# V products of two tiles in one run of TensorE, in a fused attention and MLP kernel on one Trainium2 core

## The chip, the core and the metric

The kernel runs on one core of one Trainium2 chip. The metric is the device time of one execution in microseconds (us); lower is better. The core has TensorE (PE in the profile, with its weight loads as PEld), VectorE (DVE), ScalarE (ACT), GpSimd (POOL) and SyncE (SP), which issues most DMAs. Each engine works through its own list of instructions in order, and they wait for one another by semaphores. Matrix products land in PSUM, which GpSimd does not read here; everything else lies in SBUF.

## The reference, cut to what matters

```python
q_assign = np.argmax(np.einsum('bhsd,hcd->bhsc', q_n, c_n), axis=-1)   # 16 clusters per head
k_assign = np.argmax(np.einsum('bhsd,hcd->bhsc', k_n, c_n), axis=-1)
mask = q_assign[:, :, :, None] == k_assign[:, :, None, :]
scores = np.where(mask, scale * np.matmul(q, k.transpose(0, 1, 3, 2)), -1e9)
attn = np.exp(scores - np.max(scores, axis=-1, keepdims=True))
x = np.matmul(attn / (np.sum(attn, axis=-1, keepdims=True) + 1e-09), v)
...
u = x + np.real(np.fft.fft(np.fft.fft(x, axis=1), axis=2))
un = (u - mean) / np.sqrt(var + 1e-6)
x = u + np.maximum(un @ w_ch1, 0.0) @ w_ch2                             # 512 -> 2048 -> 512
...
h = np.maximum(x @ w_in, 0.0)                                           # 512 -> 1024
out = (h * sigmoid(conv3(h))) @ w_out                                   # 3 taps along the sequence
```

There are 2 batches, 8 heads, 768 tokens and 64 columns per head. A head is masked attention over 768 keys; the batch's heads together are the 512 columns of the MLP stages.

## The kernel before

**Tiles and steps.** The 16 heads (2 batches of 8) are cut into 6 tiles of 128 rows each, 96 tiles in all. One loop of steps `n` works on all of them, skewed: step n makes the scores of tile n+8 with queries as rows (`score_max`, tiles named `s`; VectorE takes the row maxima `m6`), the transposed scores of tile n (`score_exp`, tiles named `t`; ScalarE takes the exponential `p`), splits the exponential of tile n-1 into a high f16 part (`prob_hi`, ScalarE) and a low one (`prob_lo`, GpSimd, or VectorE for the tiles in the set `LO_ON_DVE`), and multiplies tile n-3 with V (`attn_v`, 18 matmuls of 65 columns). Scores are two passes over f32 stacks `X` and `Y`, which hold a head's high and low parts, the mask rows and the maxima.

**The queue of PSUM slots.** `s` and `t` share three PSUM slots in turn, so each `s` or `t` waits until the tile three places earlier has been read: an `s` by VectorE's maximum, a `t` by ScalarE's exponential.

**What is hung into the steps.** All other work of the stage has a place in a step by a table: `at(where, step, ...)` gives the usual one and `MOVED` overrides it. The places within a step are, in this order: `pre`, `mid` (between the `s` matmuls and the maximum), `mid2` (after the `t` matmuls), `late` (before `prob_lo`), then V products, then `aft`, `post` and `fill`. For every pair of heads m (12 steps) this is: `prep_sims`, `sims_turn`, `equal_turn` and `equal_sole` make the cluster mask (matmuls, a ScalarE copy `eT`, VectorE maxima and comparisons); `prep_hi` and `prep_lo` split q and k into the tile `G`; `v_max`, `v_turn` and `v_step` scale and split V; `max_turn` (step 6h-2) transposes the maxima of head h and sends them by DMA into `Y`; `attn_out` divides by the row sums; `prep_stack` (step 6h-12) moves a head's parts from `G` into its stacks by five DMAs on SP, needed by the `s` of step 6h-8; `ahead_start`, `ahead` and `ahead_store` fetch and convert the first MLP weights. From step 52 on, the DFT of the first batch (`mixing`) and its normalisation (`norm`) are hung in too.

**The end of the stage.** After step 88 the last exponentials are split, and the first MLP weights are split into parts by `first_split(0)` to `first_split(3)` on VectorE: parts 0 and 1 (`firstEH`, `firstEL`) feed the up product `first_up`, parts 2 and 3 (`firstYsH`, `firstYsL`) the down product, which comes after both up products. The exponentials of tiles 89, 93 and 95 stay in their PSUM slot until their low part is taken (`IN_PLACE`). After this the MLP stages run, with their own order, which the change leaves alone.

Of the kernel before, what the change touches and what calls it, by code (L numbers as in the profile page):

```python
# [21 lines left out]
B, H, S, D = 2, 8, 768, 64  # L22

DFT_LOADS = (9, 20, 21, 32, 33, 44)
LO_ON_DVE = {4, 5, 6, 7, 8, 14, 16, 19, 20, 28, 31, 32, 40, 43, 44, 52, 55, 57, 59, 61, 67, 68, 72, 77, 80,
             82, 85, 88, 90, 92}
# [6 lines left out]
MOVED = {  # L33
    ("prep_sims", 2): ("post", 5),
    ("equal_turn", 2): ("mid", 7),
    ("equal_sole", 2, 0): ("mid", 8),
    ("prep_hi20", 2): ("late", 8),
    ("equal_sole", 2, 1): ("mid", 9),
    ("prep_hi21", 2): ("fill", 9),
    ("prep_lo", 2, 0): ("pre", 9),  # L40
    ("attn_out", 0, 0): ("fill", 10),
    ("attn_out", 0, 1): ("fill", 10),
    ("attn_out", 0, 2): ("fill", 11),
    ("prep_lo", 2, 1): ("late", 11),
    ("v_max", 2): ("aft", 11),
    ("v_step", 1, 0): ("late", 11),
    ("v_step", 1, 1): ("aft", 11),
    ("v_turn", 1): ("mid", 11),
    ("v_step", 1, 2): ("pre", 12),
    ("v_step", 1, 3): ("late", 12),  # L50
    ("v_step", 1, 4): ("late", 13),
    ("v_step", 1, 5): ("aft", 14),
    ("ahead_start", 0): ("fill", 15),
    ("attn_out", 1, 0): ("fill", 15),
    ("v_step", 2, 0): ("late", 15),
    ("v_turn", 2): ("mid", 15),
    ("v_step", 2, 1): ("late", 16),
    ("v_step", 2, 2): ("aft", 16),
    ("v_step", 2, 3): ("fill", 16),
    ("ahead0_1",): ("fill", 17),  # L60
    ("attn_out", 1, 2): ("pre", 17),
    ("prep_sims", 3): ("post", 17),
    ("v_step", 2, 4): ("fill", 17),
    ("prep_hi30", 3): ("late", 20),
    ("prep_hi31", 3): ("late", 20),
    ("v_step", 2, 5): ("fill", 20),
    ("prep_lo", 3, 0): ("late", 21),
    ("attn_out", 2, 1): ("late", 22),
    ("prep_lo", 3, 1): ("pre", 22),
    ("attn_out", 2, 2): ("fill", 23),  # L70
    ("ahead0_3",): ("fill", 24),
    ("v_max", 3): ("late", 25),
    ("attn_out", 3, 0): ("aft", 26),
    ("ahead_start", 1): ("aft", 27),
    ("ahead_store", 0): ("pre", 27),
    ("v_step", 3, 0): ("late", 27),
    ("v_turn", 3): ("mid", 27),
    ("attn_out", 3, 1): ("late", 28),
    ("v_step", 3, 1): ("late", 28),
    ("v_step", 3, 2): ("aft", 28),  # L80
    ("v_step", 3, 3): ("fill", 28),
    ("ahead1_1",): ("fill", 29),
    ("prep_sims", 4): ("post", 29),
    ("v_step", 3, 4): ("fill", 29),
    ("prep_hi41", 4): ("fill", 32),
    ("v_step", 3, 5): ("fill", 32),
    ("prep_lo", 4, 0): ("late", 33),
    ("attn_out", 4, 1): ("late", 34),
# [40 lines left out]
    ("row",): ("fill", 58),
    ("attn_out", 8, 2): ("fill", 59),  # L130
    ("rowL",): ("fill", 59),
    ("ahead_start", 3): ("late", 60),
# [62 lines left out]
def tile_net(ctx, tc, qk, v, cen, w12, w34, conv, dft, odd, out):  # L195
# [304 lines left out]
    with ExitStack() as actx:  # L500
# [464 lines left out]
        for i, t in enumerate((0, 3, 1, 4, 2, 5)):  # L965
            n = 73 + 3 * i
# [465 lines left out]
```

## Time and profile before

| | us |
|---|---|
| median of 3 runs (671.08 to 673.03) | 672.08 |
| time of the profiled execution | 670.07 |
| its span, first to last instruction | 668.2 |
| PE busy in the span | 655.2 (98%) |
| DVE busy | 525.4 (79%) |
| ACT busy | 424.0 (63%) |
| POOL busy | 179.7 (27%) |
| mean granted TensorE clock, share of full | 0.999 |

The profiled execution spends 1.87 us outside its span and lies 2.0 us under the median of the runs. Matmuls are pipelined in the records: one lasts about 0.34 us but the next starts 0.18 us later, so the distance between starts tells more than the busy time.

### The profile page before, as it was taken

Reading aid. Unit: us, or ns where it says so; the run is one execution under the profiler, and the core shown is the slowest. Engines: PE = TensorE matmul, PEld = TensorE weight load, DVE = VectorE, ACT = ScalarE, POOL = GpSimd, SP = SyncE. Lnnn points to the kernel's source line nnn. Section 1 sums busy time; section 2 is a strip of 40 time slices with the busy share of each in tenths; the row PEclk is TensorE's granted clock in tenths of the full one; section 3 lists DMA queues with packets and bytes.
Section 4 is the critical chain, followed back from the end, with each engine's and each line's share of the span. In section 5 each row is a group of like instructions: output and inputs, shape, how many; then the busy total and the mean of one; then the engine's idle time right before and its main releaser. Section 6 shows DMA issues by size and latency. Waiting matters only on the chain.

```text
span 668.2 us, 12652 instructions
## 1 busy us (share of the span) xinstructions
PE 655.2 (98%) x5041; PEld 486.9 (73%) x5041; DVE 525.4 (79%) x889; ACT 424.0 (63%) x686; POOL 179.7 (27%) x138
## 2 busy tenths in 40 slices
PE   8999999999999999999999999999999999999997
PEld 4888888888898888999989995555555455555553
DVE  6897888788788999996699829998533569987653
ACT  6788888978687894475256734775533466655442
POOL 8445858687569640000011000000000000000000
PEclk9999999999999999999999999999999999999999
DMA  8668887774623810334023330333000000002002
GB/s 222 164 164 207 196 222 210 189 186 100 170 76 74 225 45 2 127 136 179 1 66 124 127 127 0 127 128 126 1 1 1 0 1 1 0 1 95 1 0 95
DMA packets 21543, 65.42 MB, mean 98 GB/s; under 512 B 4438, under 2 KB 7306, under 8 KB 18668
## 3 DMA queue, kind: packets, MB, share of 16 engines
q1 hardware_dynamic: 20476, 60.86, 31.8%
q0 software_dynamic: 1008, 3.75, 2.0%
q8 instruction: 40, 0.66, 0.4%
q14 instruction: 19, 0.16, 0.1%
HBM read 40.84 MB, written 5.58 MB: 69 GB/s over the span
## 4 chain that ended last, share of the span: by engine, by line
PE 72%; DVE 15%; ACT 5%; DMA 3%; issue 2%; SPq 1%; POOL 0%; DVEq 0%; ACTq 0%; POOLq 0%
PE acc L232 8%; PE acc L231 8%; PE acc L230 8%; PE av L870 6%; PE up L230 5%; PE up L231 5%; PE up L232 5%; PE s L790 5%; PE t L830 4%; PE s L792 4%; PE t L832 4%; PE u L230 2%; PE u L232 2%; PE u L231 2%; DVE wa L1138 1%
## 5 line engine op out<-in xcount | busy, mean ns | idle before, releaser
L858 POOL TENSOR_TENSOR p<-p,p 128x768 f16<-128x768 f32 x63 | 107.6, 1718 | 57.8 <-ACT p L850 32.6
L795 DVE TENSOR_REDUCE m<-s 128x1 f32<-128x768 f32 x96 | 90.5, 947 | 17.9 <-PE s L792 7.8
L838 ACT ACTIVATE p<-t,cbias 128x768 f32<-128x768 f32 x93 | 83.6, 900 | 16.2 <-PE t L832 14.8
L850 ACT CAST p<-p 128x768 f16<-128x768 f32 x90 | 74.7, 830 | 1.1
L870 PE MATMUL av<-V,p 128*128 128x65 f16 x1728 | 70.0, 194 | 0.0
L870 PEld LDWEIGHTS <-p 128*128 128x128 f16 x1728 | 58.6, 98 | 15.1 <-issue 15.0
L790 PE MATMUL s<-X 128*128 128x384 f32 x192 | 56.2, 373 | 1.1 <-ACT X L699 0.2
L830 PE MATMUL t<-X 128*128 128x384 f32 x192 | 54.4, 364 | 0.8 <-DVE d L880 0.4
L792 PE MATMUL s<-Y 96*128 96x384 f32 x192 | 49.6, 339 | 0.0
L832 PE MATMUL t<-Y 98*128 98x384 f32 x192 | 49.5, 339 | 0.0
L230 PE MATMUL up<-un,wa 128*128 128x384 f16 x128 | 41.8, 326 | 0.5 <-ACT wa L1137 0.3
L230 PE MATMUL u<-x,wb 128*128 128x384 f16 x128 | 41.7, 326 | 0.1
L231 PE MATMUL up<-un,wa 128*128 128x384 f16 x128 | 41.7, 326 | 0.0
L232 PE MATMUL u<-x,wb 128*128 128x384 f16 x128 | 41.7, 326 | 0.0
L231 PE MATMUL u<-x,wb 128*128 128x384 f16 x128 | 41.7, 326 | 0.0
L232 PE MATMUL up<-un,wa 128*128 128x384 f16 x128 | 41.6, 326 | 0.0
L230 PE MATMUL up<-un,wha 128*128 128x384 f32 x112 | 38.0, 339 | 0.0
L231 PE MATMUL up<-un,wha 128*128 128x384 f32 x112 | 37.8, 338 | 0.0
L232 PE MATMUL up<-un,wla 128*128 128x384 f32 x112 | 37.6, 337 | 0.0
L230 PE MATMUL acc<-wb,gH 128*128 128x512 f16 x96 | 36.4, 379 | 0.2 <-ACT gH L1198 0.2
L230 PE MATMUL acc<-wa,h 128*128 128x512 f16 x96 | 36.4, 379 | 0.0
L231 PE MATMUL acc<-wa,h 128*128 128x512 f16 x96 | 36.4, 379 | 0.0
(404 smaller groups left out, 1653.0 us busy)
## 6 DMA issues: line engine op xcount, KB each, us to landing
rawa<-w SPq DMA_DIRECT2D x14, 1024.0 KB
rawb<-w SPq DMA_DIRECT2D x8, 1024.0 KB
raw<-qk SPq DMA_DIRECT2D x7, 768.0 KB
X<-G SPq DMA_DIRECT2D x13, 384.0 KB
Y<-G SPq DMA_DIRECT2D x13, 384.0 KB
vraw<-v SPq DMA_DIRECT2D x8, 384.0 KB
out<-y SPq DMA_DIRECT2D x12, 256.0 KB
X<-G SPq DMA_DIRECT2D x14, 192.0 KB
```

The lines of the kernel that those rows point to most:

```text
L230: T.matmul(o, sH, mH, start=start, stop=False)
L231: T.matmul(o, sH, mL, start=False, stop=False)
L232: T.matmul(o, sL, mH, start=False, stop=stop)
L790: T.matmul(t[:, c, 0:384], X[:, 0, sl], X[:, 1, 384 * c:384 * c + 384], start=True, stop=False)
L792: T.matmul(t[:, c, 0:384], Y[0:96, 0, sl], Y[0:96, 1, 384 * c:384 * c + 384], start=False, stop=True)
L795: V.tensor_reduce(m6s[h][:, i:i + 1], t[:, :, 0:384], AX.XY, ALU.max, negate=True)
L830: T.matmul(t[:, c, 0:384], X[:, 1, sl], X[:, 0, 384 * c:384 * c + 384], start=True, stop=False)
L832: T.matmul(t[:, c, 0:384], Y[0:98, 1, sl], Y[0:98, 0, 384 * c:384 * c + 384], start=False, stop=True)
L838: A.activation(p, t[:, :, 0:384], AF.Exp, bias=cbias, scale=0.125)
L850: A.copy(p16[:, 0], p32s[n])
L858: eng.tensor_sub(p16[:, 1], p, p16[:, 0])
L870: T.matmul(o, p16[:, k, 128 * j:128 * j + 128], v16[:, i, h % 2, 65 * part:65 * part + 65], start=(i + j + k + part == 0), stop=(i == 5), ...
```

## The change

Up to step 58 (`PAIRED`), V products run only in even steps, and there for two tiles, n-4 and n-3; odd steps have none. After step 58 each step has one tile, as before. The number of matmuls is the same. Besides, `MOVED` gives new places to some 70 small operations, `prob_lo` of tiles 5, 6 and 14 goes from VectorE to GpSimd and that of tile 53 the other way, one `v_max` goes to ScalarE, and `first_split` 1, 2 and 3 go from steps 92, 93 and 95 to 93, 96 and 96.

```diff
-LO_ON_DVE = {4, 5, 6, 7, 8, 14, 16, 19, 20, 28, 31, 32, 40, 43, 44, 52, 55, 57, ...
+LO_ON_DVE = {4, 7, 8, 16, 19, 20, 28, 31, 32, 40, 43, 44, 52, 53, 55, 57, ...
-ABS_ON_ACT = (0, 6)
+ABS_ON_ACT = (0, 1, 6)
 MOVED = {
-    ("prep_sims", 2): ("post", 5),
+    ("prep_sims", 2): ("aft", 5),
+    ("v_max", 1): ("aft", 6),
...
+    ("equal_sole", 3, 0): ("mid2", 20),
...
-    ("v_step", 2, 5): ("fill", 20),
+    ("v_step", 2, 5): ("pre", 19),
...
-    ("ahead_start", 2): ("aft", 37),
+    ("ahead_start", 2): ("aft", 35),
...
-    ("first_split", 2): ("fill", 93),
-    ("first_split", 3): ("fill", 95),
+    ("first_split", 1): ("fill", 93),
+    ("first_split", 2): ("fill", 96),
+    ("first_split", 3): ("fill", 96),
 }
...
-        LEAD, LAG = 8, 3
+        LEAD, LAG, PAIRED = 8, 3, 58
...
-            if 0 <= n - LAG < 88:
-                attn_v(n - LAG)
+            if 0 < n - LAG < 88:
+                for i in (0,) if n > PAIRED else (1, 0) if n % 2 == 0 else ():
+                    attn_v(n - LAG - i)
```

On PE, around steps 25 and 26, the V products (`av` from `p16`, weight load and matmul) stood behind every `t`. Before:

```order
L790 MATMUL s33_1337<-X2_180 128x384 x2
L792 MATMUL s33_1337<-Y2_181 128x384 x2
L830 MATMUL t25_1345<-X1_175 128x384 x2
L832 MATMUL t25_1345<-Y1_176 128x384 x2
L870 LDWEIGHTS p16_22_1266
L870 MATMUL av3_1197<-V16_1_159,p16_22_1266 128x65
L870 LDWEIGHTS p16_22_1266
L870 MATMUL av3_1197<-V16_1_159,p16_22_1266 128x65
```

With the change (its lines lie 17 further down) the same place reads:

```order
L807 MATMUL s33_1337<-X2_180 128x384 x2
L809 MATMUL s33_1337<-Y2_181 128x384 x2
L847 MATMUL t25_1345<-X1_175 128x384 x2
L849 MATMUL t25_1345<-Y1_176 128x384 x2
L807 MATMUL s34_1356<-X2_180 128x384 x2
L809 MATMUL s34_1356<-Y2_181 128x384 x2
L847 MATMUL t26_1364<-X1_175 128x384 x2
L849 MATMUL t26_1364<-Y1_176 128x384 x2
```

The scores of two steps now follow each other, and the V products of tiles 22 and 23 come behind them in one run.

On DVE, at the end of the stage (`first` tiles are the split weights, `p16_93<-t93` is the low part that frees a PSUM slot), the list was:

```order
L1006 TENSOR_TENSOR firstEL_4273<-wa0_4077,firstEH_4195 128x512
L848 CAST p16_92_4275<-p92_4252 128x768
L858 TENSOR_TENSOR p16_92_4275<-p92_4252,p16_92_4275 128x768
L878 TENSOR_SCALAR d14_4302<-av14_4095 128x6
L1008 CAST firstYsH_4304<-wa0_4077 128x512
L856 TENSOR_TENSOR p16_93_4306<-t93_4277,p16_93_4306 128x768
L880 RECIPROCAL d14_4302<-d14_4302 128x6
L848 CAST p16_94_4336<-p94_4313 128x768
L883 SCALAR_TENSOR_TENSOR U_68<-av14_4095,vsc7_3415,d14_4302 128x6x64
L1006 TENSOR_TENSOR firstYsL_4364<-wa0_4077,firstYsH_4304 128x512
```

It is now:

```order
L895 TENSOR_SCALAR d14_4300<-av14_4095 128x6
L1023 TENSOR_TENSOR firstEL_4302<-wa0_4077,firstEH_4195 128x512
L873 TENSOR_TENSOR p16_93_4304<-t93_4275,p16_93_4304 128x768
L897 RECIPROCAL d14_4300<-d14_4300 128x6
L865 CAST p16_94_4334<-p94_4311 128x768
L900 SCALAR_TENSOR_TENSOR U_68<-av14_4095,vsc7_3415,d14_4300 128x6x64
L873 TENSOR_TENSOR p16_95_4362<-t95_4336,p16_95_4362 128x768
L1034 SCALAR_TENSOR_TENSOR firste1_4385<-up0_0_4386,firste0_4384 128x384
L1025 CAST firstYsH_4401<-wa0_4077 128x512
L1023 TENSOR_TENSOR firstYsL_4403<-wa0_4077,firstYsH_4401 128x512
```

The two `firstYs` parts moved behind the low parts of tiles 93 and 95, and `firstEL` behind the cast and the low part of tile 92.

On SP, around step 35 (`mr` sends maxima, the L735 and L728 rows are `prep_stack(8)`), the fetch of MLP weights stood behind the moves:

```order
L805 DMA Y0_139<-mr6_1723 1x6x128 x2
L735 DMA X2_180<-G4_1665 64x1536
L735 DMA X2_180<-G4_1665 32x2x768
L735 DMA Y2_181<-G4_1665 32x2x768
L728 DMA X2_180<-ohd4_1681 16x12x128
L735 DMA Y2_181<-G4_1665 64x2x768
L519 DMA raw5_1798<-qk 128x1536
L981 DMA ahead_950<-w12 128x512
```

It now stands ahead of them:

```order
L822 DMA Y0_139<-mr6_1704 1x6x128 x2
L998 DMA ahead_931<-w12 128x512
L752 DMA X2_180<-G4_1628 64x1536
L752 DMA X2_180<-G4_1628 32x2x768
L752 DMA Y2_181<-G4_1628 32x2x768
L745 DMA X2_180<-ohd4_1680 16x12x128
L752 DMA Y2_181<-G4_1628 64x2x768
L536 DMA raw5_1781<-qk 128x1536
```

The row `ahead<-w12` moved past the five moves of head 8 and past the load of the next q and k.

## Rows read from the trace of the kernel before

**Rows 1.** Page, part 1: busy time, share of span, instructions of each engine.

```profile
PE 655.2 (98%) x5041; PEld 486.9 (73%) x5041; DVE 525.4 (79%) x889; ACT 424.0 (63%) x686; POOL 179.7 (27%) x138
```

**Rows 2.** Windows: stretch, its us, busy PE, PEld, DVE, ACT, POOL, PEclk, DMA, GB/s.

```profile
60.33:156.69 96.36, 94.55 (x1136) 80.99 (x1134) 79.03 (x120) 82.68 (x113) 70.81 (x48) 1.00 0.76 190
239.34:258.83 19.49, 18.19 (x263) 16.22 (x263) 18.16 (x30) 14.68 (x21) 6.42 (x5) 1.00 0.01 3
```

**Rows 3.** Timeline of PE: start, us, what; steps without and with V products.

```profile
24.39 0.52 PE L790 MATMUL s<-X 128*128 128x384 f32 x2
24.75 0.52 PE L792 MATMUL s<-Y 96*128 96x384 f32 x2
...
81.43 0.73 PE L870 MATMUL av<-V,p 128*128 128x65 f16 x18
82.00 0.60 PE L790 MATMUL s<-X 128*128 128x384 f32 x2
82.44 0.51 PE L792 MATMUL s<-Y 96*128 96x384 f32 x2
```

**Rows 4.** Timeline of PE: two tiles' V products in one run, step 95.

```profile
250.62 1.29 PE L870 MATMUL av<-V,p 128*128 128x65 f16 x36
```

**Rows 5.** Timeline, PE and DVE, where PE starts late in steps 18 to 23.

```profile
62.97 0.73 PE L870 MATMUL av<-V,p 128*128 128x65 f16 x18
63.83 0.58 PE L790 MATMUL s<-X 128*128 128x384 f32 x2
...
71.05 0.52 PE L792 MATMUL s<-Y 96*128 96x384 f32 x2
71.74 0.27 PE L800 MATMUL s<-ident,m 128*6 128x128 f32 x1 [0.17 <-DVE m L795]
...
73.40 0.94 DVE L795 TENSOR_REDUCE m<-s 128x1 f32<-128x768 f32 x1
73.55 0.52 PE L792 MATMUL s<-Y 96*128 96x384 f32 x2
74.49 0.59 PE L830 MATMUL t<-X 128*128 128x384 f32 x2 [0.42 <-DVE d L880]
```

**Rows 6.** Timeline, steps 19 to 21: the mask's copy, the maximum, V's low half.

```profile
64.59 0.39 PE L661 MATMUL s<-ident,eq 128*96 128x128 f16 x4
...
65.07 0.58 ACT L664 COPY eT<-s 96x512 f16<-96x512 f16 x1 [0.39 <-PE s L661]
...
65.69 0.96 DVE L795 TENSOR_REDUCE m<-s 128x1 f32<-128x768 f32 x1 [1.14 <-ACT eT L664]
...
69.40 1.01 DVE L772 SCALAR_TENSOR_TENSOR V<-vraw,vsc,V 128x768 f16<-128x768 f32 x1
```

**Rows 7.** Chain that ended last in 60 to 120 us: start, us, what.

```profile
63.07 6.08 DMA Y<-G
```

**Rows 8.** Timeline of PE: last score of step 35, first scores of head 8.

```profile
102.95 0.52 PE L832 MATMUL t<-Y 98*128 98x384 f32 x2
...
112.37 0.60 PE L790 MATMUL s<-X 128*128 128x384 f32 x2
112.98 0.59 PE L792 MATMUL s<-Y 96*128 96x384 f32 x2
```

**Rows 9.** Timeline of DVE, end of the stage.

```profile
247.54 0.68 DVE L432 TENSOR_TENSOR un<-unT,un 128x512 fp32r<-128x512 f32 x1
248.14 1.55 DVE L1006 TENSOR_TENSOR firstEL<-wa,firstEH 128x512 fp32r<-128x512 f32 x1
...
251.15 0.42 DVE L1008 CAST firstYsH<-wa 128x512 fp32r<-128x512 f32 x1
251.48 0.95 DVE L856 TENSOR_TENSOR p<-t,p 128x768 f16<-128x768 f32 x1
```

**Rows 10.** Timeline of POOL and PE in the same stretch.

```profile
247.49 1.65 POOL L858 TENSOR_TENSOR p<-p,p 128x768 f16<-128x768 f32 x1 [4.55 <-ACT p L850]
...
252.58 0.42 PE L230 MATMUL up<-un,firstEH 128*128 128x384 f32 x1 [0.67 <-DVE d L880]
```

More of the change, by code (lines that the diff above doesn't have):

```diff
@@ L24 @@
 DFT_LOADS = (9, 20, 21, 32, 33, 44)
-LO_ON_DVE = {4, 5, 6, 7, 8, 14, 16, 19, 20, 28, 31, 32, 40, 43, 44, 52, 55, 57, 59, 61, 67, 68, 72, 77, 80,
-             82, 85, 88, 90, 92}
+LO_ON_DVE = {4, 7, 8, 16, 19, 20, 28, 31, 32, 40, 43, 44, 52, 53, 55, 57, 59, 61, 67, 68, 72, 77, 80, 82, 85,
+             88, 90, 92}
 AHEAD = 4
@@ L31 @@
 LO_BY_DVE = ()
-ABS_ON_ACT = (0, 6)
+ABS_ON_ACT = (0, 1, 6)
 MOVED = {
-    ("prep_sims", 2): ("post", 5),
+    ("prep_sims", 2): ("aft", 5),
+    ("v_max", 1): ("aft", 6),
     ("equal_turn", 2): ("mid", 7),
-    ("equal_sole", 2, 0): ("mid", 8),
+    ("equal_sole", 2, 0): ("mid2", 8),
     ("prep_hi20", 2): ("late", 8),
+    ("prep_lo", 2, 0): ("fill", 8),
     ("equal_sole", 2, 1): ("mid", 9),
-    ("prep_hi21", 2): ("fill", 9),
-    ("prep_lo", 2, 0): ("pre", 9),
+    ("prep_hi21", 2): ("late", 9),
     ("attn_out", 0, 0): ("fill", 10),
@@ L43 @@
     ("attn_out", 0, 2): ("fill", 11),
-    ("prep_lo", 2, 1): ("late", 11),
+    ("prep_lo", 2, 1): ("pre", 11),
     ("v_max", 2): ("aft", 11),
@@ L49 @@
     ("v_step", 1, 2): ("pre", 12),
-    ("v_step", 1, 3): ("late", 12),
+    ("v_step", 1, 3): ("pre", 12),
     ("v_step", 1, 4): ("late", 13),
@@ L54 @@
     ("attn_out", 1, 0): ("fill", 15),
-    ("v_step", 2, 0): ("late", 15),
+    ("v_step", 2, 0): ("aft", 15),
     ("v_turn", 2): ("mid", 15),
@@ L59 @@
     ("v_step", 2, 3): ("fill", 16),
+    ("ahead0_0",): ("late", 17),
     ("ahead0_1",): ("fill", 17),
-    ("attn_out", 1, 2): ("pre", 17),
-    ("prep_sims", 3): ("post", 17),
+    ("prep_sims", 3): ("aft", 17),
     ("v_step", 2, 4): ("fill", 17),
+    ("ahead0_2",): ("aft", 18),
+    ("attn_out", 1, 2): ("pre", 18),
+    ("v_step", 2, 5): ("pre", 19),
+    ("equal_sole", 3, 0): ("mid2", 20),
     ("prep_hi30", 3): ("late", 20),
     ("prep_hi31", 3): ("late", 20),
-    ("v_step", 2, 5): ("fill", 20),
-    ("prep_lo", 3, 0): ("late", 21),
-    ("attn_out", 2, 1): ("late", 22),
+    ("prep_lo", 3, 0): ("fill", 21),
+    ("attn_out", 2, 1): ("pre", 22),
     ("prep_lo", 3, 1): ("pre", 22),
-    ("attn_out", 2, 2): ("fill", 23),
-    ("ahead0_3",): ("fill", 24),
+    ("ahead0_3",): ("aft", 23),
+    ("attn_out", 2, 2): ("late", 23),
+    ("ahead_start", 1): ("aft", 25),
     ("v_max", 3): ("late", 25),
     ("attn_out", 3, 0): ("aft", 26),
-    ("ahead_start", 1): ("aft", 27),
-    ("ahead_store", 0): ("pre", 27),
-    ("v_step", 3, 0): ("late", 27),
+    ("attn_out", 3, 1): ("late", 27),
+    ("v_step", 3, 0): ("aft", 27),
     ("v_turn", 3): ("mid", 27),
-    ("attn_out", 3, 1): ("late", 28),
     ("v_step", 3, 1): ("late", 28),
@@ L81 @@
     ("v_step", 3, 3): ("fill", 28),
+    ("ahead1_0",): ("late", 29),
     ("ahead1_1",): ("fill", 29),
-    ("prep_sims", 4): ("post", 29),
+    ("prep_sims", 4): ("aft", 29),
     ("v_step", 3, 4): ("fill", 29),
[L85 to L88, printed above, removed]
+    ("ahead1_2",): ("aft", 30),
+    ("ahead_store", 0): ("fill", 30),
+    ("v_step", 3, 5): ("pre", 31),
+    ("equal_sole", 4, 0): ("mid2", 32),
+    ("prep_hi41", 4): ("late", 32),
+    ("prep_hi40", 4): ("aft", 33),
+    ("attn_out", 4, 1): ("pre", 34),
+    ("prep_lo", 4, 0): ("fill", 34),
     ("prep_lo", 4, 1): ("pre", 34),
-    ("attn_out", 4, 2): ("fill", 35),
-    ("ahead1_3",): ("fill", 36),
-    ("ahead_start", 2): ("aft", 37),
-    ("v_max", 4): ("late", 37),
+    ("ahead1_3",): ("aft", 35),
+    ("ahead_start", 2): ("aft", 35),
+    ("attn_out", 4, 2): ("late", 37),
+    ("v_max", 4): ("aft", 37),
     ("attn_out", 5, 0): ("aft", 38),
-    ("v_step", 4, 0): ("late", 39),
+    ("ahead_store", 1): ("fill", 39),
+    ("v_step", 4, 0): ("aft", 39),
     ("v_turn", 4): ("mid", 39),
@@ L100 @@
     ("v_step", 4, 3): ("fill", 40),
+    ("ahead2_0",): ("late", 41),
     ("ahead2_1",): ("fill", 41),
-    ("ahead_store", 1): ("fill", 41),
-    ("prep_sims", 5): ("post", 41),
+    ("prep_sims", 5): ("aft", 41),
     ("v_step", 4, 4): ("fill", 41),
-    ("v_step", 4, 5): ("fill", 44),
+    ("ahead2_2",): ("aft", 42),
+    ("v_step", 4, 5): ("pre", 43),
+    ("equal_sole", 5, 0): ("mid2", 44),
+    ("prep_hi50", 5): ("late", 44),
+    ("attn_out", 6, 1): ("pre", 45),
     ("prep_hi51", 5): ("fill", 45),
-    ("prep_lo", 5, 0): ("late", 45),
-    ("attn_out", 6, 1): ("late", 46),
+    ("prep_lo", 5, 0): ("fill", 45),
     ("prep_lo", 5, 1): ("pre", 46),
-    ("attn_out", 6, 2): ("fill", 47),
-    ("ahead2_3",): ("fill", 48),
-    ("v_max", 5): ("late", 49),
+    ("ahead2_3",): ("aft", 47),
+    ("attn_out", 6, 2): ("late", 47),
+    ("v_max", 5): ("fill", 49),
     ("attn_out", 7, 0): ("aft", 50),
-    ("ahead_store", 2): ("aft", 51),
-    ("v_step", 5, 0): ("late", 51),
+    ("ahead_store", 2): ("fill", 51),
+    ("v_step", 5, 0): ("aft", 51),
     ("v_turn", 5): ("mid", 51),
@@ L120 @@
     ("v_step", 5, 3): ("fill", 52),
-    ("even0",): ("aft", 53),
+    ("v_step", 5, 4): ("fill", 52),
+    ("even0",): ("fill", 53),
+    ("even1",): ("fill", 53),
     ("prep_sims", 6): ("fill", 53),
-    ("v_step", 5, 4): ("fill", 53),
-    ("even1",): ("fill", 54),
+    ("v_step", 5, 5): ("pre", 54),
+    ("prep_hi60", 6): ("late", 56),
     ("prep_lo", 6, 0): ("fill", 56),
-    ("v_step", 5, 5): ("fill", 56),
+    ("attn_out", 8, 0): ("late", 57),
+    ("even",): ("fill", 57),
+    ("row",): ("aft", 57),
     ("attn_out", 8, 1): ("late", 58),
     ("prep_hi61", 6): ("late", 58),
[L129 to L132, printed above, removed]
+    ("attn_out", 8, 2): ("late", 59),
+    ("rowL",): ("late", 59),
     ("odd0",): ("aft", 60),
     ("odd1",): ("fill", 60),
+    ("ahead_start", 3): ("fill", 61),
     ("attn_out", 9, 0): ("aft", 62),
@@ L139 @@
     ("attn_out", 9, 1): ("late", 64),
-    ("oddL",): ("aft", 64),
-    ("ahead3_3",): ("fill", 65),
+    ("oddL",): ("fill", 64),
+    ("ahead3_3",): ("aft", 65),
     ("v_step", 6, 0): ("late", 66),
     ("v_step", 6, 1): ("aft", 66),
-    ("v_step", 6, 2): ("aft", 66),
     ("v_turn", 6): ("mid", 66),
+    ("v_step", 6, 2): ("aft", 67),
     ("v_step", 6, 3): ("aft", 67),
     ("v_step", 6, 4): ("aft", 67),
+    ("ahead_store", 3): ("fill", 68),
+    ("attn_out", 10, 1): ("fill", 68),
     ("prep_hi71", 7): ("fill", 68),
     ("z1L",): ("pre", 68),
-    ("ahead_store", 3): ("fill", 69),
     ("ab0A",): ("late", 71),
@@ L158 @@
     ("v_turn", 7): ("mid", 72),
-    ("ab0M",): ("fill", 73),
+    ("ab0M",): ("pre", 73),
+    ("ab1M",): ("fill", 73),
     ("scale", 0): ("pre", 73),
@@ L162 @@
     ("v_step", 7, 3): ("aft", 73),
-    ("ab1M",): ("fill", 74),
     ("attn_out", 11, 0): ("fill", 74),
```

## The prediction

> **What bounds it now.** I read the page's totals first: PE is busy 655.2 of 668.2 us, the next engine, DVE, 79% [rows 1]. Only what shortens PE's own work, or takes away a wait of PE, can pay. The share is an average, so I went on to the stage that the change touches. In 60.33 to 156.69 us, which are steps of the loop, PE has 94.55 us of records in 96.36, at the full clock; ACT has 82.68, DVE 79.03, POOL 70.81, and the DMA engines move 190 GB/s [rows 2]. PE binds, but three engines and the transfers are close enough that any queue of theirs can stop it for half a microsecond. At the stage's end (239.34 to 258.83) PE lacks 1.3 us and DVE is as full as PE, 18.16 against 18.19 [rows 2], so there the order of DVE's list decides.
>
> Next I read PE's timeline by distances between starts, since one record outlasts the start of the next. A pair of score matmuls takes 0.36 us (24.39 to 24.75) where scores or other f32 matmuls stand ahead, and 0.44 (82.00 to 82.44) behind V products [rows 3]. A V run of 18 takes 0.57 to the next start (81.43 to 82.00) [rows 3]. Its record lasts 0.73, that of 36 matmuls 1.29 [rows 4], so a second tile in the same run adds 0.56: the same price, with no seam inside.
>
> Then I looked for places where these distances are longer. One V run takes 0.86 (62.97 to 63.83), one score pair 0.69 (71.05 to 71.74), another 0.94 (73.55 to 74.49) [rows 5]. The last two end on DVE: the transpose of the maxima waits for `m`, and the `t` matmul waits for the maximum that starts at 73.40 [rows 5].
>
> **The change, part by part.**
>
> **A, the paired V products.** Even steps from 4 to 58 keep a V run, 28 of them; the 28 between lose theirs, and with it one slow entry into the scores. Each is worth 0.44 - 0.36 = 0.08 us, in all 28 x 0.08 = 2.2 us. The matmuls stay the same in number, and by rows 4 the longer run costs nothing of its own. As the starts are rounded to 0.01, one entry is worth 0.06 to 0.10: 1.7 to 2.8. Rows of the same kind are shown both ways, so I take 2.2.
>
> **B, the waits in the steps.** Removed, if all goes well: in the cycle of 12 steps that rows 5 come from, 0.86 - 0.57 = 0.29, 0.69 - 0.35 = 0.34 and 0.94 - 0.35 = 0.59, together 1.22. A run of 1.13 us in front of every second step is more cover than the 0.57 that stood there. Steps 4 to 58 are 4.5 such cycles, so at best 5.5 us go.
>
> Created: odd steps have no cover at all. The three slots turn, so `t` of step 20 needs the slot of `s` of step 19 (tile 27), which DVE's maximum empties. Before, that `s` starts at 63.83, and the maximum ends at 65.69 + 0.96 = 66.65, 2.82 us later, because it must wait for ScalarE's copy `eT` [rows 5, 6]. PE now reaches `t` after three pairs of about 0.71 (2.13) and the mask's transposes, at most 0.39 [rows 6]: it waits 0.3 to 0.7. Next, `equal_sole` moves behind the `t` matmuls (`mid2`) of step 20, and the maximum of that step behind it; this costs nothing up to one pair, 0.7. Third, the low half of V, 1.01 us on DVE, stands now at the head of step 19, ahead of that maximum. DVE was idle 1.14 us there [rows 6], enough to hide it if the V data are there in time; without that cover it costs 1.01. So a cycle gets back 0.3 to 2.4, four cycles (steps 8, 20, 32, 44) 1.2 to 9.6. Against the 5.5 this is a net of -4.3 to +4.1. Rows 6 speak for the half-hidden case (the idle time is there, the wait for `eT` too), about 1.3 a cycle, which is what the removed waits were. I take B as nothing and keep both ends.
>
> The other moves go with B. Single `ahead` casts, `attn_out`, `v_max` and `prep_lo` change places within a step or two; their engines have 14% (ACT), 18% (DVE) and 27% (POOL) of slack in rows 2, and only what stands ahead of a maximum or an exponential reaches PE. Tiles 5, 6 and 14 give their low part to POOL (1.65 us there, [rows 10]), which is idle 25 us of the 96 [rows 2]: nothing.
>
> **C, the end.** Before, the up product starts at 252.58, 0.67 us late, released by DVE [rows 10]. It needs a PSUM slot that the low part of tile 93 frees; that part starts at 251.48 and ends at 252.43, and ahead of it stand `firstYsH` (0.33 to the next start) and `firstEL` (1.55) [rows 9]. A subtraction of the same shape a moment earlier takes 0.68 [rows 9]; `firstEL` ran while POOL worked from 247.49 to 249.14 [rows 10]. After the change `firstYsH` stands behind, and `firstEL` comes later. If it then runs alone, 0.33 + 0.87 = 1.2 leaves the path; if it stays slow, 0.33. But PE has 36 V matmuls from 250.62 on, 1.29 long less the 0.17 or so by which records overlap [rows 4], until about 251.75, so it can't start before: at most 252.58 - 251.75 = 0.83 comes back. I take 0.8 (bounds 0.3 and 0.83). The second up product waits for the same chain, so nothing gives this back before the down product, for which the two `firstYs` parts still come in time: they are 0.4 and at most 1.55 of DVE against the two up products.
>
> The Trainium skill, "SBUF — State Buffer", section "Who interferes with whom", says that a VectorE instruction with two SBUF inputs and a GpSimd instruction that reads SBUF exclude each other, and that the second to start stands still until the first is done. By that rule the slow `firstEL` is the time up to POOL's end, and 0.8 stands if POOL is idle at its new place; the trace agrees, as `firstEL` ends at 249.69, 0.55 after POOL's instruction.
>
> **D, the transfers.** A head's stacks are free after its last `t` user, five steps before its first `s`. For head 8 that span was 103.47 (102.95 + 0.52) to 112.98, 9.51 us, and the second matmul there started 0.61 behind the first and not 0.44 [rows 8]: the moves of `Y` landed last. One of them takes 6.08 at another head [rows 7]. Five V runs lay in that span, now two double ones: 0.57 less, and three slow entries fewer, 0.24, so 0.81 less time to land. Besides, a fetch of 512 KB now goes ahead of head 8's moves; at 190 GB/s [rows 2] it is 2.8 us of the engines. Packets of several transfers share them, so its cost lies between 0 and 2.8. In the forecast D costs nothing beyond what B's middle holds, as only head 8 shows a late landing.
>
> **Sum.** 2.2 + 0 + 0.8 = 3.0 less: from the profiled 670.07 to 667.1. That execution lies 2.0 under the median, so on the median's scale 672.08 - 3.0 = 669.1. A difference of 0.3%, 2.0 us, is about what a measurement of this kernel can tell: 670.1 and 674.1 bound "same".
>
> **The rivals.** *All the old waits go and the new ones hide*: 5.5 more, 663.6. For it: the 1.14 idle of DVE in rows 6, and a cover twice as long. Against it: `eT` keeps its place and ScalarE its load of 86%.
>
> *The loops outside PE set the pace*: the moves of four heads (2, 4, 6, 8) need their 9.5 us whatever PE does, so each takes 0.81 back, 3.2 in all, more than A saves. Only the end's 0.8 arrives: 671.3, no change that can be told. For it: rows 8. Against it: rows 2, where the transfers still have a quarter of their time.
>
> *Slower, by landing late*: the fetch delays head 8's moves by its full 2.8, and each of four heads lacks 0.81: 2.8 + 3.2 = 6.0 lost, 3.0 saved, 675.1. It decides once head 8's last move lands some 12 us after `t` of step 35, against 9.5 now. For it: the fetch stands ahead in the same queue. Against it: 190 GB/s is what the engines move at a busy share of 0.76 [rows 2], so the fetch can in part use time that was free. The Trainium skill, "DMA: Bandwidth & Descriptors", section "Queues, rings and completion order", says that each engine takes the descriptors of one issuer in the order of its ring; by that the full 2.8 counts, and the time would be this rival's. No row of before shows the two in this order.
>
> **How the numbers follow.** The forecast gets 0.48 (own range 667 to 671: A and the end's bounds, B within 1.5 either way; 0.40 of it faster, 0.08 same). All waits gone: 0.16, faster. Loops: 0.24, same. Slower: 0.12. So faster 0.56, same 0.32, slower 0.12. For the range I leave out the slower rival and the fastest half of the 663.6 case: 664.8 to 672.0.
>
> **What would show it.** Right: score pairs at 0.36 in odd steps and 28 entries of 0.44 fewer; `up` starting near 251.75 behind the V run, with the stage's other times taken off. Wrong: `t` of steps 20, 32 and 44 released late by DVE's `m` for more than 1 us (then B is a loss); the `Y` matmul of head 8's first score released by DMA (then the loops or the slower rival); no gap over 0.3 left in steps 8 to 58 (then 663.6); `firstEL` still at 1.55, or the down product waiting for `firstYs` (then C shrinks). If a V run of 36 takes more than 1.15 to the next start, A is wrong.

## The result and the profile after

The changed kernel takes 677.58 us (median of 10 executions, 672.82 to 679.16) against 671.76 us before (10 executions, 670.16 to 673.03): 1.0084 times the time before, 95% interval 1.0065 to 1.0102, so slower by 0.84%. The forecast was 669.1 with a range up to 672.0; the outcome lies above it. The profiled execution took 674.59 us, its span is 672.9 us against 668.2.

First, busy time (the same part of the page as [rows 1]):

```profile
PE 655.8 (97%) x5041; PEld 489.1 (73%) x5041; DVE 525.8 (78%) x886; ACT 423.9 (63%) x688; POOL 183.6 (27%) x140
```

PE does the same work and is busy 0.6 us longer, while the span grows by 4.7 us, so most of the loss is idle time of PE; the rest is a stretch at a slower clock, shown below. Where the time goes is seen from the start of the same step's scores in both traces:

| scores of step | before, us | after, us | after minus before |
|---|---|---|---|
| 2 | 24.39 | 24.42 | 0.02 |
| 38 | 108.04 | 108.09 | 0.05 |
| 39 | 110.10 | 110.64 | 0.54 |
| 40 | 112.37 | 113.09 | 0.73 |
| 41 | 114.80 | 119.12 | 4.32 |
| 42 | 117.75 | 121.50 | 3.75 |
| 74 | 206.28 | 210.11 | 3.83 |
| 76 | 211.97 | 216.88 | 4.91 |
| first up product | 252.58 | 257.17 | 4.59 |

At the scores of an even step up to 58 the changed kernel has done the V products of one tile fewer, 0.57 us of work, so odd steps and those after 58 compare like with like. Three places stand out: instead of a gain there is a loss of 0.5 us up to step 39, 3.8 us are lost around head 8's first scores (between those of steps 39 and 41), and 1.1 us in step 75. The waits of PE from 20 to 162 us (who waited, for whom, total, times, longest):

```profile
PE s L809 <- DMA Y<-G: 1.6, 1, 1.6
PE t L847 <- DVE m L812: 1.6, 5, 0.6
PE s L807 <- DMA X<-ohd: 0.6, 1, 0.6
PE s L807 <- ACT p L855: 0.5, 1, 0.5
PE s L817 <- DVE m L812: 0.5, 1, 0.5
PE s L807 <- DVE eq L650: 0.4, 1, 0.4
```

**Head 8.** The timeline of PE there answers to [rows 8]:

```profile
111.99 0.51 PE L849 MATMUL t<-Y 98*128 98x384 f32 x2
113.09 0.59 PE L807 MATMUL s<-X 128*128 128x384 f32 x2 [0.59 <-DMA X<-ohd]
115.31 0.98 PE L809 MATMUL s<-Y 96*128 96x384 f32 x2 [1.63 <-DMA Y<-G]
...
116.16 0.99 PE L847 MATMUL t<-X 128*128 128x384 f32 x2
116.94 0.84 PE L849 MATMUL t<-Y 98*128 98x384 f32 x2
117.58 1.70 PE L887 MATMUL av<-V,p 128*128 128x65 f16 x36
```

PE stands still 0.59 and 1.63 us, both for moves of head 8's stacks. Then its instructions themselves are longer: a pair of score matmuls 0.98 instead of 0.59, the V run 1.70 instead of the 1.29 of [rows 4]. The stretches (columns as in [rows 2]) say why:

```profile
112.00:113.00 1.00, 0.50 (x3) 0.18 (x2) 1.00 (x2) 0.40 (x1) 1.00 (x1) 1.00 1.17 220
113.00:115.30 2.30, 0.59 (x2) 0.32 (x3) 0.00 (x0) 0.50 (x1) 1.76 (x2) 0.96 0.95 264
115.30:116.20 0.90, 0.89 (x4) 0.70 (x4) 0.00 (x0) 0.00 (x0) 0.00 (x0) 0.50 0.93 369
116.20:118.50 2.30, 2.30 (x22) 1.99 (x21) 1.64 (x7) 1.61 (x3) 0.84 (x1) 0.50 0.11 41
118.50:120.00 1.50, 1.50 (x29) 1.50 (x27) 0.43 (x1) 1.11 (x2) 0.81 (x1) 0.99 0.01 2
```

Behind the wait the granted clock (third column from the right) is 0.50, 1.2 GHz in place of 2.4, for 3.4 us, and then full again. Between the two waits PE had one score pair. In the same microseconds the DMA engines are busy all the time (share 0.93 to 1.17). SP's rows show what was among their work:

```profile
103.24 0.41 SPq L998 DMA_DIRECT2D ahead<-w  x1
103.76 1.35 SPq L752 DMA_DIRECT2D X<-G  x2
105.20 1.81 SPq L752 DMA_DIRECT2D Y<-G  x1
107.11 1.54 SPq L745 DMA_DIRECT2D X<-ohd  x1
108.69 1.18 SPq L752 DMA_DIRECT2D Y<-G  x1
```

The fetch of weights goes out half a microsecond ahead of the moves. The last move, issued at 108.69, is waited for until 115.31. In the kernel before, the last move and the fetch went out as follows, and this stretch of its windows, in which the moves were under way, shows the DMA engines busy throughout (share 1.02) with the fetch still behind:

```profile
106.84 0.92 SPq L735 DMA_DIRECT2D Y<-G  x1
...
109.76 0.44 SPq L981 DMA_DIRECT2D ahead<-w  x1
```

```profile
107.00:112.00 5.00, 5.00 (x64) 4.53 (x63) 4.44 (x5) 3.90 (x5) 4.86 (x4) 1.00 1.02 231
```

**Step 75.** GpSimd's low parts of p (two in this row, the first until 215.22), VectorE's low half of V, and what follows:

```profile
213.57 3.96 POOL L875 TENSOR_TENSOR p<-p,p 128x768 f16<-128x768 f32 x2
213.62 2.42 DVE L789 SCALAR_TENSOR_TENSOR V<-vraw,vsc,V 128x768 f16<-128x768 f32 x1 [1.29 <-ACT V L787]
...
216.37 0.41 DVE L385 TENSOR_TENSOR m<-ab,m 128x258 f32<-128x258 f32 x1
...
216.88 0.59 PE L807 MATMUL s<-X 128*128 128x384 f32 x2 [0.92 <-ACT p L855]
```

VectorE started 0.05 us behind GpSimd and took 2.42 us. Before, the same instruction of this step took 1.17:

```profile
209.80 1.17 DVE L772 SCALAR_TENSOR_TENSOR V<-vraw,vsc,V 128x768 f16<-128x768 f32 x1 [1.30 <-ACT V L770]
```

Behind it on VectorE comes the sum at 216.37, which empties a DFT product (`ab`) that holds the next of the three PSUM slots. It ends at 216.78, and PE, which waits 0.92 us, starts at 216.88; the exponential that the row names was over at 216.33.

**The end**, DVE's rows that answer to [rows 9]:

```profile
252.47 0.68 DVE L449 TENSOR_TENSOR un<-unT,un 128x512 fp32r<-128x512 f32 x1
253.12 1.36 DVE L865 CAST p<-p 128x768 f16<-128x768 f32 x1
254.52 0.96 DVE L875 TENSOR_TENSOR p<-p,p 128x768 f16<-128x768 f32 x1
...
255.47 0.68 DVE L1023 TENSOR_TENSOR firstEL<-wa,firstEH 128x512 fp32r<-128x512 f32 x1
256.07 0.95 DVE L873 TENSOR_TENSOR p<-t,p 128x768 f16<-128x768 f32 x1
...
257.04 0.52 DVE L865 CAST p<-p 128x768 f16<-128x768 f32 x1
```

and GpSimd and PE beside them, which answer to [rows 10]:

```profile
252.42 1.65 POOL L875 TENSOR_TENSOR p<-p,p 128x768 f16<-128x768 f32 x1 [4.54 <-ACT p L867]
...
257.17 0.41 PE L247 MATMUL up<-un,firstEH 128*128 128x384 f32 x1 [0.35 <-DVE d L897]
```

`firstEL` now takes 0.68, as forecast, but the cast that took its place beside GpSimd's instruction takes 1.36 (the one at 257.04, alone, 0.52). The wait of the up product shrank from 0.67 to 0.35 and not to nothing.

### The profile page after: what moved, and what is told of

It is laid out like the page before. It is cut to its first block, busy times and chain, and to the rows that moved or that the text cites. A ratio compares the mean times of both kernels' runs of the same rounds, so it can differ in the third digit from the quotient of the medians.

```text
span 672.9 us, 12649 instructions
## 1 busy us (share of the span) xinstructions
PE 655.8 (97%) x5041; PEld 489.1 (73%) x5041; DVE 525.8 (78%) x886; ACT 423.9 (63%) x688; POOL 183.6 (27%) x140
## 3 DMA queue, kind: packets, MB, share of 16 engines
q0 software_dynamic: 1008, 3.75, 2.0%
## 4 chain that ended last, share of the span: by engine, by line
PE 72%; DVE 16%; ACT 5%; DMA 3%; issue 2%; SPq 1%; POOL 0%; ACTq 0%; POOLq 0%; DVEq 0%
PE acc L249 8%; PE acc L248 8%; PE acc L247 8%; PE av L887 6%; PE up L247 5%; PE up L249 5%; PE up L248 5%; PE s L807 4%; PE t L847 4%; PE s L809 4%; PE t L849 3%; PE u L247 2%; PE u L249 2%; PE u L248 2%; DVE m L812 2%
## 5 line engine op out<-in xcount | busy, mean ns | idle before, releaser
L875 POOL TENSOR_TENSOR p<-p,p 128x768 f16<-128x768 f32 x65 | 112.1, 1736 | 67.6 <-ACT p L867 33.8
L887 PE MATMUL av<-V,p 128*128 128x65 f16 x1728 | 65.3, 194 | 0.0
L807 PE MATMUL s<-X 128*128 128x384 f32 x192 | 54.6, 365 | 2.8 <-ACT p L855 1.4
L807 PEld LDWEIGHTS s<-X 128*128 128x128 f32 x192 | 30.7, 189 | 8.4 <-issue 2.2
L809 PEld LDWEIGHTS s<-Y 96*128 96x128 f32 x192 | 35.1, 190 | 2.0 <-issue 1.9
```

The costliest lines, as they stand in the source:

```text
L807: T.matmul(t[:, c, 0:384], X[:, 0, sl], X[:, 1, 384 * c:384 * c + 384], start=True, stop=False)
L809: T.matmul(t[:, c, 0:384], Y[0:96, 0, sl], Y[0:96, 1, 384 * c:384 * c + 384], start=False, stop=True)
```

## Experiments

Theory 1: the fetch of 512 KB shares the DMA engines with head 8's moves and makes them late; the wait lets the clock fall, and both together are most of the loss. Theory 2: the pairing itself, by the shorter span for the moves and the steps without cover, is the loss. Each kernel ran beside the kernel before on the same chip; ratios are to that, with the 95% interval.

**1. The fetch back** (to the changed kernel):

```diff
-    ("ahead_start", 2): ("aft", 35),
+    ("ahead_start", 2): ("aft", 37),
```

> The changed kernel with one edit: the third fetch of MLP weights (512 KB) goes back from step 35 to step 37, behind the five stack moves of head 8. Theory 1 (the fetch is what makes head 8 late): the wait of TensorE at head 8's first scores shrinks from 0.6 + 1.6 us to under 0.7, the granted clock stays at 1.0 all through, and the time falls by 3 to 4 us, from 677.6 to about 674. Theory 2 (the span between the last use of a stack and its first use has become too short by itself): the wait stays over 1.5 us, the clock still drops, and the time stays at 676 to 678.

672.52 us, ratio 1.002 (1.001 to 1.003): of 0.84%, 0.64% is gone, some 4.3 us. The clock in the profile is full but for the last 2.1 us of the kernel. Head 8's `Y` is still late, but by 0.61 us only; head 6's is late too, by 0.55. Theory 1 holds.

**2. The fetch alone forward** (to the kernel before):

```diff
-    ("ahead_start", 2): ("aft", 37),
+    ("ahead_start", 2): ("aft", 35),
```

> The kernel before with one edit: the same fetch goes forward from step 37 to step 35, ahead of head 8's moves. Theory 1: head 8's second score matmul waits 1.5 to 2.5 us for a move of Y, the granted clock falls to half for some 3 us behind it, and the time is 2 to 4 us over that of before (674 to 676). Theory 2: the longer span of the unpaired steps takes it in, under 1 us more (672 to 673).

675.66 us, ratio 1.0074 (1.0055 to 1.0093). One edit makes nearly the whole loss, without any pairing. PE's rows and the clock behind them:

```profile
114.00 0.59 PE L790 MATMUL s<-X 128*128 128x384 f32 x2 [1.28 <-DMA X<-ohd]
115.88 0.98 PE L792 MATMUL s<-Y 96*128 96x384 f32 x2 [1.30 <-DMA Y<-G]
```

```profile
116.00:120.60 4.60, 4.60 (x29) 4.10 (x30) 2.07 (x7) 2.72 (x4) 1.65 (x1) 0.50 0.18 62
120.60:122.00 1.40, 1.40 (x7) 1.09 (x7) 1.15 (x2) 0.00 (x0) 0.00 (x0) 0.50 0.08 22
```

Against the trace of before, the scores of step 38 start 0.19 us later and those of step 44 5.63 us later: 5.4 us at one place, of which the two waits are 2.6. The `Y` matmul itself starts 2.9 us later than before (115.88 against 112.98 in [rows 8]).

**3. The wait filled, fetch forward** (to experiment 2; useless matmuls on head 7's stack, whose result the real ones overwrite):

```diff
+            for j in range(12 if n == 48 else 0):
+                T.matmul(t[:, j % 2, 0:384], Xs[1][:, 0, sl], Xs[1][:, 1, 0:384], start=True, stop=True)
```

> The kernel before with the fetch ahead of head 8's moves (675.7 in its own run), and 12 matmuls of 384 columns whose result is thrown away in front of head 8's first scores, about 2.1 us of work inside the 2.6 us in which TensorE waits there. Theory (half of the loss is the clock that falls after the wait): the clock stays at 1.0, the wait itself stays, and the time falls by some 3 us to about 672.8, although TensorE does more. Rival (the clock has nothing to do with the wait, or the matmuls cost their own 2.1 us): 675.7 to 677.8.

674.86 us, ratio 1.0072 (1.0052 to 1.0092). In the profile the clock stays full, head 8's `Y` comes at 115.89 as before (115.88), and the following scores are 0.59 long again: the V run of step 42 starts 2.9 us later than in the kernel before, where experiment 2 is 5.6 behind. But the median hardly moved, where 672.8 was expected: this execution lost 0.9 us in step 64 to another wait (the load of V came late at ScalarE), and six executions from 674.21 to 678.37 tell little. So I repeated it on the changed kernel.

**4. The wait filled, in the changed kernel** (the same two lines):

> The changed kernel, and 12 matmuls of 384 columns with a result that is thrown away in front of head 8's first scores, about 2.2 us. If some 1.5 to 3 us of the loss are the clock that falls behind the wait: the clock of the profile is 1.0 at 110 to 125 us, and the time falls from 677.6 to 674.5 to 676. If the clock has no part in it: 677 to 679.

675.39 us, ratio 1.0051 (1.0034 to 1.0067) against 1.0084: 2.2 us less time with 2.2 us more work, though the intervals touch.

```profile
112.35 2.24 PE L807 MATMUL s<-X 128*128 128x384 f32 x12
114.43 0.51 PE L809 MATMUL s<-X 128*128 128x384 f32 x2
115.58 0.59 PE L811 MATMUL s<-Y 96*128 96x384 f32 x2 [0.64 <-DMA Y<-G]
```

```profile
112.00:116.00 4.00, 3.37 (x19) 2.99 (x19) 1.01 (x2) 0.91 (x1) 2.80 (x2) 1.00 0.98 257
116.00:120.00 4.00, 4.00 (x58) 3.26 (x56) 3.15 (x9) 2.94 (x5) 1.66 (x1) 1.00 0.12 42
```

`Y` lands about when it did (115.58 against 115.31), the clock is 1.00 throughout. By the medians about half of the fetch's 4.3 us is the clock; by the traces it is 1.2 of 3.3 us here (between the scores of steps 39 and 43) and 2.4 of 5.4 from experiment 2 to 3. So a third to a half is an estimate, and the medians alone don't prove it.

**5. The fetch from another issuer** (to experiment 2):

```diff
-            nc.sync.dma_start(out=raw.bitcast(I64), in_=w12[f][:, 512 * i:512 * i + 512])
+            (G if q == 2 else nc.sync).dma_start(out=raw.bitcast(I64), in_=w12[f][:, 512 * i:512 * i + 512])
```

> The kernel before with the fetch at step 35, but issued by GpSimd and not by SyncE. If its place ahead of the moves in SyncE's order is what delays them: they land as in the kernel before (112.9), no wait over 0.3 us, 671.5. If it is the sharing of the DMA engines in these microseconds: a wait of 1.5 to 2.5 us and a clock at half for some 3 us, as with SyncE (675.7).

677.46 us, ratio 1.0079 (1.0058 to 1.01). SP now issues the moves as before (from 103.23 on), with nothing ahead of them. GpSimd sends the fetch only when four of the five moves are out, and yet they are later still:

```profile
106.28 0.57 POOL L981 DMA_DIRECT2D ahead<-w  x1
```

```profile
PE s L790 <- DMA X<-ohd: 2.1, 1, 2.1
PE s L792 <- DMA Y<-G: 1.6, 1, 1.6
```

So it doesn't take a place ahead in SP's list, as the prediction's rival had it; the sharing of the engines in these microseconds is enough. The Trainium skill, "DMA: Bandwidth & Descriptors", section "Queues, rings and completion order", says besides that each engine takes turns between the queue rows that have work for it. That fits this run, though the turns themselves aren't shown; the rule of order within one ring doesn't explain it.

**6. Half of the fetch forward** (to the kernel before; columns 0 to 255 at step 35, the others at step 37):

```diff
+            nc.sync.dma_start(out=raw.bitcast(I64), in_=w12[1][:, 0:256])
...
+        at(aft, 35, ahead_half)
```

> The kernel before with half of the fetch (256 KB) at step 35 ahead of the moves and the other half at step 37 behind them. If the delay goes with the bytes: half of the wait of the full fetch, 1.2 to 1.4 us in place of 2.6. If the clock falls only behind a longer wait, it stays at 1.0 and the time is 672.5 (1.2 more than before); if it falls behind this one too, 674.

671.64 us, ratio 0.9996 (0.9974 to 1.0019). PE waits 0.76 us for `Y` and not at all for `X`, less than half of the 2.6, the clock stays full, and in the time nothing can be told.

**7. ab0M and ab1M back** (to the changed kernel):

```diff
-    ("ab0M",): ("pre", 73),
-    ("ab1M",): ("fill", 73),
+    ("ab0M",): ("fill", 73),
+    ("ab1M",): ("fill", 74),
```

> The changed kernel with one edit: ab0M and ab1M (additions of the DFT's result around step 73) go back to the places that they had before. Theory 1: GpSimd is then not in a low part (1.65 us) when VectorE starts the low half of V in step 75; that instruction takes 1.2 us and not 2.4, TensorE's wait of 1.1 us behind it goes, and the time falls by about 1.1 us to 676.5. Theory 2: the two engines meet at another instruction and the wait moves: within 0.3 us of 677.6.

676.61 us, ratio 1.0075 (1.0057 to 1.0093), by itself not apart from 1.0084. In the profile the low half of V takes 1.18 us and the wait in step 75 is gone, while this execution lost 1.1 us in step 64 and, with the fetch still forward, 6.8 us of it ran at a clock of 0.50. The next run is clearer.

**8. Both back** (the edits of 1 and 7):

```diff
+    ("ahead_start", 2): ("aft", 37),
+    ("ab0M",): ("fill", 73),
+    ("ab1M",): ("fill", 74),
```

> The changed kernel with two edits: the third fetch of MLP weights back behind head 8's moves (step 37), and ab0M and ab1M back to their old places. If the two costs add (the fetch alone gave 672.5 against 671.1 of the kernel before; the low half of V beside GpSimd in step 75 is 1.1 us): 671.4, no difference to the kernel before that can be told. If GpSimd's collision with VectorE only moves elsewhere: 672.5.

671.49 us, ratio 1.0004 (0.9992 to 1.0017). Within this interval, these two places are the whole loss; the 0.16% from 1.002 to here is 1.1 us, as step 75 shows, though the two intervals overlap. What is left, the pairing with the other moves, is worth nothing that can be told.

**9. Pairing alone** (to the kernel before; the `attn_v` lines of the change, no other):

```diff
+        LEAD, LAG, PAIRED = 8, 3, 58
```

> The kernel before with one edit: V products are paired up to step 58, every other operation stays where it was. If pairing by itself is worth its 28 slow entries and the old places suit it: 2.2 us faster, 669.6. If odd steps without cover bring as many waits as the pairing saves, as the trace of the changed kernel says up to step 38: within 1 us of 671.8, with waits of TensorE for VectorE's maximum in the steps of the mask. If the span for the stack moves is what counts, head 8 waits more than 1 us and the time is over 674.

673.39 us, ratio 1.0032 (1.0019 to 1.0045): slower. The waits of PE from 20 to 162 us, of which the kernel before had 0.7 for the maxima in the first row and none for these DMAs:

```profile
PE s L800 <- DVE m L795: 2.0, 5, 0.4
PE s L792 <- DMA Y<-G: 1.4, 2, 0.7
PE s L790 <- DMA X<-ohd: 0.7, 1, 0.7
```

The waits for moves are those of heads 2 (0.68, for `X`), 6 (0.70) and 8 (0.71), close to the 0.81 that the prediction's rival *the loops outside PE set the pace* put on each of four heads: 2.1 us in all, about what A was to win.

**10. The other moves alone** (experiment 8 with `PAIRED = 0`, single runs in every step):

```diff
-        LEAD, LAG, PAIRED = 8, 3, 58
+        LEAD, LAG, PAIRED = 8, 3, 0
```

> The changed kernel with the fetch and ab0M, ab1M back, and V products single in every step as before: what is left are the other moved operations and first_split. If these pay by themselves: under 670.5. If they only suit the pairing: 671 to 673, no better than the paired version's 671.5.

671.76 us, ratio 1.0004 (0.9991 to 1.0017). The moves are neutral without the pairing, and with it they make up for what it costs (1.0032 to 1.0004).

**11. The mask's operations back** (to experiment 8; `v_step` to its old place in four cycles, `equal_sole` to its usual one in three; one cycle is shown):

```diff
-    ("equal_sole", 3, 0): ("mid2", 20),
-    ("v_step", 2, 5): ("pre", 19),
+    ("v_step", 2, 5): ("fill", 20),
```

> As the run before, and besides the mask's sum (equal_sole) of heads 6 to 11 and V's low half go back to their old places in four cycles. Theory 1 (these two moves create the waits of t in steps 8, 20, 32 and 44, 0.4 each): the waits go, 1 to 1.6 us less, 670. Theory 2 (the t of an odd-even pair waits for the maximum because no V run stands in between, wherever the small operations are): the four waits of about 0.4 stay, or others of 0.3 to 0.6 take their place, as in the kernel that has only the pairing, and the time is 671 to 673.

672.51 us, ratio 1.0026 (1.0015 to 1.0038): slower than with them. The waits of `t` in steps 20, 32 and 44, 0.25 us each in experiment 8, go, as theory 1 had it; but the transposes of the maxima in steps 22, 34, 46 and 58 now wait 0.33 to 0.60, 1.8 us in all, as they do with the pairing alone. So theory 2 holds in its second form: others take their place. It fits that each of these steps stands behind one without cover.

**12. Runs in odd steps** (to experiment 8; the division steps of seven heads follow one step later; cut to the loop):

```diff
-                for i in (0,) if n > PAIRED else (1, 0) if n % 2 == 0 else ():
+                for i in (0,) if n > PAIRED or n == LAG else (1, 0) if n % 2 else ():
```

> The changed kernel with the fetch and ab0M, ab1M back at their old places, and with the runs of 36 V matmuls in odd steps (from 5 to 57) in place of even ones; the first division steps of seven heads follow one step later. Theory 1 (the waits come from the steps that lost their cover): the span between the last t of a head and the first scores of the head three on then holds three runs of 36 and not two, the moves of heads 6 and 8 land in time, the t of steps 20, 32 and 44 finds its maximum done, and the time is 2 to 3 us under the even version's 671.5: 669. Theory 2 (any pairing leaves half of the steps to wait, at other places): 671 to 673.

677.23 us, ratio 1.0092 (1.0071 to 1.0114). My theory was wrong. No stack move is late any more, as expected from three long runs in the span, but VectorE is (20 to 162 us):

```profile
PE s L810 <- DVE eq L653: 4.4, 5, 1.5
PE t L850 <- DVE m L815: 2.0, 4, 0.5
PE s L695 <- DVE m L815: 1.4, 4, 0.4
```

**13. Odd steps with the old places** (to the kernel before with `first_split` moved and the same first division steps one step later; cut to the loop):

```diff
+                for i in (0,) if n > PAIRED or n == LAG else (1, 0) if n % 2 else ():
```

> The kernel before with the three moved first_split, and with the runs of 36 in odd steps; the small operations stay at their old places. Theory 1: 28 slow entries less and no late moves, 668 to 669.5. Theory 2: new waits for VectorE's maxima of 2 us and more in all, 670.5 to 673.

675.97 us, ratio 1.0077 (1.0055 to 1.0099). Also slower; its largest waits of PE are for VectorE.

**14. The split weights alone** (to the kernel before):

```diff
+    ("first_split", 1): ("fill", 93),
-    ("first_split", 2): ("fill", 93),
-    ("first_split", 3): ("fill", 95),
+    ("first_split", 2): ("fill", 96),
+    ("first_split", 3): ("fill", 96),
```

> The kernel before with the three moved first_split alone. The prediction's step C: the up product starts 0.8 us sooner, 670.3 against 671.1. The other theory, from the trace of the changed kernel: GpSimd's low part of 1.65 us then falls on VectorE's cast of the next tile, which grows from about 0.55 to 1.36 us in place of the split, so that only 0.3 to 0.4 us comes back: 670.8, within 0.1%.

670.16 us, ratio 1.0 (0.998 to 1.002); one of its twelve executions took 677.7 at a mean clock of 0.996 and widens the interval, so the time decides nothing. The profile does: the cast beside GpSimd takes 1.37 us, `firstEL` 0.68, and the up product still waits 0.4 us. The collision moved, it didn't go.

**15. The maximum of |V| one step later** (to experiment 14):

```diff
-    ("v_max", 6): ("late", 63),
+    ("v_max", 6): ("late", 64),
```

> The kernel before with the three moved first_split and with the maximum of |V| on ScalarE for heads 12 and 13 one step later (64), because in some executions it waits in ScalarE's queue for the load of V and holds up the DFT's row behind it by 1 us. If that is the source of the spread from 670 to 672.5: median 669.8, spread under 1.5 us without disturbed runs. If not: as the kernel with first_split alone, 670.2.

670.89 us (670.24 to 671.8), ratio 1.0001 (0.9988 to 1.0014). No gain; the spread is 1.6 us, where 1.5 or less was expected, so whether the late load is its source stays open. None of the 15 kernels is faster than the kernel before by more than its interval.

## Why the prediction was wrong

**A held.** After the change a score pair behind f32 matmuls takes 0.35 us (99.69 to 100.04), and a V run of 36 takes 1.14 to the next start (101.28 to 102.42), against a limit of 1.15. The distances are those of the prediction; the 2.2 us that they add up to no run shows by itself, since every pairing brought waits with it.

**B, taken as nothing, was a loss.** Up to step 39, 18 of the 28 pairs should have won 18 x 0.08 = 1.4 us; the changed kernel is 0.54 behind there, so B cost about 2.0. The created wait was sized rightly: `t` of step 20 starts 2.87 us after the scores that it needs to be read (64.00 to 66.87), and 0.76 behind the matmul ahead of it (66.11) instead of 0.35, so 0.41 late, within the 0.3 to 0.7. It stayed far under the 1 us that was named as the sign of a loss, and B was a loss all the same. I reckoned only with that step as uncovered and let its cost cancel against the old waits; experiments 9 and 11 show that waits at the old places come back or grow. A and B together are the nothing of experiment 8.

**C was mis-sized**: 0.32 of 0.8 (0.67 to 0.35). I followed the slow instruction and not what made it slow. GpSimd's 1.65 us stayed where it was, and the next VectorE instruction fell into it. The prediction's condition, that GpSimd be idle at the new place, held for `firstEL` (0.68) and not for the cast that moved up.

**D failed, and it decided.** The prediction wrote that "D costs nothing beyond what B's middle holds, as only head 8 shows a late landing". In the trace of before head 8 was the only head whose moves had no slack, and the fetch was moved onto just those: in place of nothing it cost 4.3 us (experiment 1), by two waits and the clock behind them. The bounds of 0 and 2.8 were about right for the landing, 2.9 later in experiment 2. The argument against a high price took a mean busy share of 0.76 over 96 us [rows 2] as free time, but while these moves were under way the share was 1.02. The rival *slower, by landing late* was the right case, at a chance of 0.12 and a time of 675.1, but right by luck in its sum: of the three other heads that it charged 0.81 each, none waits for a move in the changed kernel's trace; a fetch outside SP's order delays the moves as much (experiment 5); and the clock, a third to a half of the price, was not in it. The shorter span for the moves, D's other part, shows with the pairing alone (heads 2, 6 and 8 in experiment 9), as the rival *loops* had it. The moves landed some 11 us behind `t` of step 35 (104.1 to 115.2), where the rival said that 12 decide.

**Not foreseen at all**: `ab0M` and `ab1M` changed GpSimd's order in step 75. All the prediction said on GpSimd's new work was its idle share ("nothing"); what counted was at which moment it is busy beside VectorE. This cost 1.1 us.

Still open is why the executions of the changed kernel spread so far (672.82 to 679.16). The execution at 672.82 shows a mean clock of 1.000, the five above 678 show 0.994 to 0.995, which fits a clock that falls for a shorter or longer stretch from one execution to the next, or not at all. Of this kernel only the execution at 674.59 has a trace, with 3.4 us at 0.50; that of experiment 7, which keeps the fetch, took 677.25 with 6.8 us at 0.50.

## What to carry to other kernels

Before a transfer is moved, look for the wait nearest to it that is already ended by a DMA: there these 512 KB cost 2.6 us of waits and a slow clock from one issuer and more from the other, half of them 0.76 us of wait, while two steps later the same fetch left no wait over 0.61 there. Read the busy share of the DMA engines in those microseconds and not over the stage. A wait of TensorE costs its own length, and it can cost a slow clock behind it as well; where it can't be avoided, work put into it may pay even if it is useless, as the medians of experiment 4 suggest. Where VectorE is slow beside GpSimd, try to move GpSimd's instruction: that worked in step 75, while reordering VectorE at the end of the stage only picked another victim.

## What the runs showed of the hardware

The granted clock fell to 0.50 for 3.4 us behind waits of 0.59 and 1.63 us with one score pair in between, and for 6.8 us behind 1.28 and 1.30 us; behind single waits of 0.61, 0.76 and 1.14 us it stayed at 1.00. With 2.2 us of matmuls in the first wait it stayed at 1.00 too, although 0.64 us of waiting was left.

Where the low half of V starts 0.25 to 1.6 us before the end of a low part on GpSimd, it ends 0.82 us after that end, whenever it started: so in six places of the changed kernel's trace, with lengths from 1.07 to 2.42 us (in step 75 at 216.04, GpSimd at 215.22). For `firstEL` in the kernel before that time is 0.55 (249.69 after 249.14), for the cast at the end 0.41 (254.48 after 254.07). Each is 0.1 to 0.2 less than the instruction takes alone (1.01, 0.68, 0.52), much as if VectorE stood still until then. Not every instruction does: the subtraction at 252.47, with one input in PSUM, starts 0.05 us behind GpSimd and takes its usual 0.68. The Trainium skill, "SBUF — State Buffer", section "Who interferes with whom", names casts among the VectorE instructions that can exclude GpSimd; the trace agrees, 1.36 us beside GpSimd against 0.52 alone.
